# More row maxima computed in the projections of an attention block, and key tiles with W first

## The chip, the cores and the metric

The kernel runs on one core of one Trainium2 chip. The metric is the device time of one execution in microseconds (us), here the median of three runs. A core has TensorE (PE: matmuls; PEld: its weight loads), VectorE (DVE), ScalarE (ACT), GpSimd (POOL), and SyncE (SP), which here only issues DMAs. Each engine works through its own instructions in the order in which the program lists them and waits at semaphores for the others.

## The reference

A transformer block on 2048 tokens of width 640, in float32: attention with 32 heads of width 20, then a gated feed-forward net of width 1728, each behind a layer norm and with a residual.

```
qkv = layernorm(x) @ wqkv                       # 640 x 1920
scores = q @ k.T * 20**-0.5                     # per head, 2048 x 2048
h = x + (softmax(scores) @ v) @ wo
out = h + (silu(z @ w_gate) * (z @ w_up)) @ w_down      # z = layernorm(h)
```

The softmax needs, for every query and head, the maximum of its scores over all 2048 keys. The kernel computes each score twice: once for the maximum alone, with queries as rows, and once for the exponential, with keys as rows.

## The kernel before

Tokens are worked in 4 chunks of 512 (NC), heads in 8 groups of 4 (NG). A unit u = (group g, chunk c) is one group's heads for the 512 queries of one chunk; there are 32 units.

**Maxima.** A maximum item is (u, kc, t, pair): the queries of unit u, tile t of 128 queries, two heads (pair), against the 512 keys of chunk kc. There are three forms:

- `max_pair` (L171, "wide, direct"): two matmuls, one on rows 0 to 63 and one on rows 64 to 127 of the array, write one two-bank tile ps_wide; VectorE reduces it in one instruction (L180).
- `max_halves` (L182, "wide, of halves"): the keys in it have been stored as second half (256) and difference of the halves. Two matmuls (L188) write ps_wide, ScalarE takes the Relu of one half into the tile "over" (L193), and VectorE adds, reduces and reads its accumulator, twice (L195). max(a, b) is b + relu(a - b), so that VectorE reads half as many columns of scores. The queries and keys are tiles "raw" that are loaded from DRAM for it.
- `max_one` (L200, "single"): one matmul (L204) into ps_max and one reduction (L210) for one head.

`in_projections` (L243) decides which items are computed as wide ones while the projections run: 208 of 1024 pairs. The other 816 pairs, "rest" (L254), become 1632 single ones in attention.

**Projections.** 18 slots for each of 4 chunks (L556 on): 10 "block" slots and 8 "value" slots. A block slot (`query_key`, L437) multiplies 15 times (L443) into a ps_one for 128 columns of keys or queries; `keep` (L468) stores them. `keep` copies from PSUM with ScalarE (L484); for key blocks of chunks 0 and 1 POOL makes the difference of the halves (L486); then `split` (L84) makes the high part with ScalarE (L85) and the low part with POOL (L86). `store` (L431) issues the DMAs of the block before on ScalarE's queue (L434 in the profile's rows). A value slot (`value`, L502) multiplies 15 times with 320 columns (L510); in later value slots `flip` (L410) transposes the next chunk's tokens. Chunks 0 to 2 do keys, queries, values (chunk 0 mixes keys and queries); chunk 3 does keys, values, queries.

`visit(n)` (L366) takes up to n wide maxima from two lists, "urgent" and "early", whose heads are ready; an item of halves is ready two slots after its tiles were loaded. Before, a block slot of chunks 1 to 3 visits one in its middle (L448), and every slot visits three at its end (L583). `stage` (L308) lists the tiles to be loaded, `load_items` (L313) loads them into four buffers, `staged_keys` (L325) makes the list of maxima for one group, chunk and key chunk.

**Attention.** 32 units x 16 key tiles of 128 keys, 512 tiles in all. A tile has four scores (`scores`, L943: matmul L948 into ps_one, exponential L954) and one weighing (`weigh`, L956: eight records at L958, 32 columns of the array for each of four heads), which takes the exponentials of two tiles before. ORDER writes out by hand what a tile issues: s and S are scores on the lower and the upper half of the array's rows, m and M single maxima on these halves, W the weighing with small work that hangs on it (the transposed maxima of a closed unit, `max_finish`, the preparation of weights on POOL, in the last units parts of the output projection). ps_one has four banks here, ps_max three, acc one. Before, ORDER has three entries, with 5, 3 and 2 maxima: 10 in three tiles. When no single maximum is left, a tile is "sSsSW". The maxima of a unit must be closed before its first scores, because the negated maximum rides as two more rows of its queries.

After attention come the rest of the output projection and the feed-forward net, from about 1531 us to the end; the change does not touch them.

Of the kernel before, what the change touches and what calls it, by code (L numbers as in the profile page):

```python
# [37 lines left out]
LOWEST = -3.4028234e38  # L38
GD = G * DH

ORDER = ("SmsSMMsWMm", "SsSmWmMs", "SssMWmS")


@with_exitstack
def tile_block(ctx: ExitStack, tc: tile.TileContext, x, wqkv, wo, wg, wu, wd, out):
# [136 lines left out]
    def max_halves(mx, q, k, pair, t, kc):  # L182


        ps = ps_wide()
        for b in range(2):
            rows = slice(b * ROW, b * ROW + NPART)
            nc.tensor.matmul(  # L188
                ps[:, b, :], q[rows, pair, t * P : (t + 1) * P], k[rows, pair, :],
                start=True, stop=True,  # L190
            )
        over = evp.tile([P, 2, CH // 2], F32, name="over")
        nc.scalar.activation(over, ps[:, :, CH // 2 :], AF.Relu)  # L193
        for b in range(2):
            nc.vector.tensor_tensor_reduce(  # L195
                over[:, b], ps[:, b, : CH // 2], over[:, b], 1.0, LOWEST, ALU.add, ALU.max,
                mx[:, b, pair, t, kc : kc + 1],
            )
# [44 lines left out]
    def in_projections(u, kc, t):  # L243


        g, c = divmod(u, NC)
        if u == 0 or (u == 2 and kc < 2) or (c < 2 and kc == 0):
            return True
        return c == 1 and kc == 1 and t < (2 if g < NG // 2 else 3)

    def moved(u, kc):
        return [t for t in range(TPC) if in_projections(u, kc, t)]
# [23 lines left out]
    with tc.tile_pool(name="pa", bufs=2) as pa:  # L276
# [46 lines left out]
                items[n][3:] = t, slot[0]  # L323

        def staged_keys(g, c, kc):  # L325
            k, q = place[1, g, (c, kc)], place[0, g, c]

            def one(t, pair):
                max_halves(mxs[g * NC + c], items[q][3], items[k][3], pair, t, kc)
                for n in (k, q):  # L330
                    users[n] -= 1
                load_items()

            def ready():
                return all(items[n][3] is not None and slot[0] >= items[n][4] + 2 for n in (k, q))

            pairs = [(t, pair) for t in moved(g * NC + c, kc) for pair in range(2)]
            for n in (k, q):
                users[n] += len(pairs)
            return [(ready, lambda a=a: one(*a)) for a in pairs]  # L340
# [12 lines left out]
        for g in range(1, NG):  # L353
            stage((0, 0), 1, g, 0)
            stage(0, 0, g, 0)
        for g in range(1, NG):
            stage((1, 0), 1, g, 0)
            stage(1, 0, g, 1)
            stage((1, 1), 1, g, 1)
        urgent = [a for kc in range(NC) for a in in_unit(0, kc, 18 * kc + 7)]  # L360
        early = [a for g in range(1, NG) for a in staged_keys(g, 0, 0)]
        early += in_unit(1, 0, 28) + in_unit(1, 1, 28)
        early += [a for g in range(1, NG) for kc in range(2) for a in staged_keys(g, 1, kc)]
        early += in_unit(2, 0, 46) + in_unit(2, 1, 46)

        def visit(n):  # L366
# [70 lines left out]
        def query_key(c, m):  # L437

            z_hi, z_lo = zs[c]
            ps = ps_one()  # L440
            for n, (a, w) in enumerate(((z_hi, w_hi), (z_lo, w_hi), (z_hi, w_lo))):
                for k in range(ND):
                    nc.tensor.matmul(  # L443
                        ps, w[:, k, m * P : (m + 1) * P], a[:, k, :],
                        start=(n == 0 and k == 0), stop=(n == 2 and k == ND - 1),
                    )
                    if n == 1 and k == 3 and c:
                        visit(1)  # L448
            keep(c, m, ps)

        firsts = []

        def first_blocks(*hns):

# [12 lines left out]

        def keep(c, m, ps):  # L468

            e = next_e()  # L470
            which, half, n = 1 - m % 2, CH // 2, CH
            hi, lo = e[:, 0], e[:, 1]
            copy = lo.bitcast(F32)
# [1 line left out]
            if slot[0] < 8:  # L475
                split(ps, hi[:, :CH], lo[:, :CH], nc.vector)
                if which:
                    nc.scalar.activation(over, ps[:, half:], AF.Copy)
                    nc.vector.tensor_tensor(
                        out=over, in0=ps[:, :half], in1=over, op=ALU.subtract  # L480
                    )
                    split(over, hi[:, CH:], lo[:, CH:], nc.gpsimd)
            else:
                nc.scalar.activation(copy[:, :CH], ps, AF.Copy)  # L484
                if which and c < 2:
                    nc.gpsimd.tensor_tensor(  # L486
                        out=over, in0=copy[:, :half], in1=copy[:, half:CH], op=ALU.subtract
                    )
                    n = EW
                split(copy[:, :n], hi[:, :n], lo[:, :n], nc.gpsimd)  # L490
            n = EW if which and c < 2 else CH
            r0 = m // 2 * P
            pieces, r = [], r0
# [8 lines left out]
        def value(c, t, half):  # L502
# [5 lines left out]
            for a, w in ((z_hi, w_hi), (z_hi, w_lo), (z_lo, w_hi)):  # L508
                for k in range(ND):
# [2 lines left out]
                        start=(n == 0), stop=(n == 3 * ND - 1),  # L512
                    )
                    n += 1
            dst = ev[:, half * 4 : half * 4 + 4, : G * VW].rearrange("p g (h w) -> p g h w", h=G)
            nc.scalar.activation(
                dst[:, :, :, :DH], ps.rearrange("p (g h d) -> p g h d", g=4, h=G), AF.Copy
# [38 lines left out]
        for c in range(NC):  # L556
# [7 lines left out]
            for j, (kind, *which) in enumerate(work):  # L564
# [11 lines left out]
                if which:  # L576
# [3 lines left out]
                            keep(0, m, ps)  # L580
                    else:
                        (query_key if kind == "block" else value)(c, *which)
                visit(3)  # L583
                if c == 0 and j == 6:
                    for ev in evs:
                        nc.gpsimd.memset(ev, 1.0)
# [439 lines left out]
    for u in range(NU):  # L1026
# [4 lines left out]
        for kt in range(NT):  # L1031
# [1 line left out]
            ready = [v for v, at in closing.items() if at == now[0]]  # L1033
            probs = [pp.tile([P, 2, CH], F32, name="probs") for _ in range(2)]
            heads = [[0, 2], [1, 3]]
            order = ORDER[now[0] % 3] if singles[0] or singles[1] else "sSsSW"
            for op in order:
                if op in "mM":
                    next_max(int(op == "M"))
# [618 lines left out]
```

## Time and profile before

| | us |
|---|---|
| median of three runs (2119.76 to 2120.84) | 2120.24 |
| the profiled execution | 2118.48 |
| its span | 2116.7 |
| projections, to the first score of attention | 346.26 |
| attention, from there to its last parts | to about 1531 |
| output projection's rest and feed-forward net | from there |

How to read the rows: a group is "line, engine, operation, out<-in, shape, xcount | busy us, mean ns of one | idle time of the engine just before them, and what ended it". Busy time is the union of the instructions' times, so that busy time over count is less than the mean where they overlap. A row of a stretch has its bounds and length, then the busy time and the number of instructions of each engine, the granted clock of TensorE as a share, the DMA engines' share and the GB/s. A row of the order of time has start, length, engine, line, operation, tiles, how many were merged, and in brackets the idle time before and what ended it. "ACTq" is an instruction of ScalarE's sequencer, such as the issue of a DMA. The ends of matmuls are modelled, so that TensorE's busy share counts little; its starts are used.

### The profile page before, as it was taken

Reading aid. Unit: us, or ns where it says so; the run is one execution under the profiler, and the core shown is the slowest. Engines: PE = TensorE matmul, PEld = TensorE weight load, DVE = VectorE, ACT = ScalarE, POOL = GpSimd, SP = SyncE. Lnnn points to the kernel's source line nnn. Section 1 sums busy time; section 2 is a strip of 40 time slices with the busy share of each in tenths; the row PEclk is TensorE's granted clock in tenths of the full one; section 3 lists DMA queues with packets and bytes.
Section 4 is the critical chain, followed back from the end, with each engine's and each line's share of the span. In section 5 each row is a group of like instructions: output and inputs, shape, how many; then the busy total and the mean of one; then the engine's idle time right before and its main releaser. Section 6 shows DMA issues by size and latency. Waiting matters only on the chain.

```text
span 2116.7 us, 36528 instructions
## 1 busy us (share of the span) xinstructions
PE 2077.2 (98%) x12636; PEld 1207.4 (57%) x12636; DVE 1695.8 (80%) x3355; ACT 1381.2 (65%) x2727; POOL 707.1 (33%) x1013
## 2 busy tenths in 40 slices
PE   7989999999999999999999999999999999999999
PEld 5756665333333333333333333335578888888888
DVE  6676767999999999999999999996458766666677
ACT  4645655999999899989999999995753222212221
POOL 2222212234334333443430001001135535663456
PEclk9999999999999999999999999999999999999999
DMA  8564543333342533434332213123137745784542
GB/s 261 182 207 148 164 127 90 118 102 128 118 147 81 173 102 120 159 131 142 123 134 60 48 32 91 36 80 96 35 117 246 276 161 200 287 313 154 187 163 94
DMA packets 194159, 297.95 MB, mean 141 GB/s; under 512 B 46840, under 2 KB 81656, under 8 KB 192952
## 3 DMA queue, kind: packets, MB, share of 16 engines
q1 hardware_dynamic: 180392, 266.77, 38.9%
q10 hardware_dynamic: 13584, 28.85, 4.5%
q8 instruction: 101, 1.65, 0.3%
q14 instruction: 82, 0.67, 0.1%
HBM read 196.44 MB, written 98.30 MB: 139 GB/s over the span
## 4 chain that ended last, share of the span: by engine, by line
PE 89%; DVE 4%; DMA 2%; ACT 2%; POOL 1%; issue 1%; ACTq 1%; SPq 0%; POOLq 0%; DVEq 0%
PE acc L958 24%; PE ps_one L948 15%; PE ps_a L1121 15%; PE ps_max L204 15%; PE ps_b L1215 8%; PE ps_one L443 4%; PE ps_one L510 3%; PE ps_max L686 2%; PE ps_wide L188 1%; PE ps_b L686 1%; DVE mx L180 1%; DVE over L195 1%; DVE mx L210 1%; PE ps_wide L176 1%; ACT over L193 1%
## 5 line engine op out<-in xcount | busy, mean ns | idle before, releaser
L954 ACT ACTIVATE probs<-ps_one 128x512 f32<-128x512 f32 x2048 | 1045.3, 621 | 131.4 <-PE ps_one L948 126.5
L210 DVE TENSOR_REDUCE mx<-ps_max 128x1 f32<-128x512 f32 x1632 | 1021.2, 683 | 95.0 <-PE ps_max L204 53.1
L948 PE MATMUL ps_one<-q_stk,k_stk 62*128 62x512 f32 x2048 | 550.1, 421 | 0.7 <-ACT e L484 0.7
L958 PE MATMUL acc<-probs,v_stk 128*32 128x512 f32 x4096 | 545.2, 604 | 0.3
L204 PE MATMUL ps_max<-k_stk,q_stk 60*128 60x512 f32 x1632 | 540.9, 460 | 2.3 <-DVE mx L210 1.5
L204 PEld LDWEIGHTS ps_max<-k_stk,q_stk 60*128 60x128 f32 x1632 | 230.2, 184 | 427.9 <-DVE mx L210 410.3
L948 PEld LDWEIGHTS ps_one<-q_stk,k_stk 62*128 62x128 f32 x2048 | 299.8, 185 | 81.1 <-ACT probs L954 51.5
L1336 DVE TENSOR_TENSOR tmp<-ps_a,tmp 128x512 f32<-128x512 f32 x208 | 141.3, 690 | 120.2 <-PE ps_a L1121 94.5
L1215 PE MATMUL ps_b<-halves,yp 128*128 128x320 f32 x1032 | 179.4, 308 | 2.0 <-POOL yp L86 1.2
L1215 PEld LDWEIGHTS ps_b<-halves,yp 128*128 128x128 f32 x1032 | 165.1, 188 | 18.6 <-POOL yp L86 1.5
L195 DVE CUSTOM_DVE_ANT_0 over<-ps_wide,over 128x256 f32<-128x256 f32 x296 | 109.7, 420 | 82.1 <-ACT over L193 79.6
L958 PEld LDWEIGHTS acc<-probs,v_stk 128*32 128x32 f32 x4096 | 80.6, 108 | 159.7 <-issue 151.7
L221 POOL CAST both<-neg 128x16 fp32r<-128x16 f32 x32 | 6.6, 208 | 470.1 <-DVE neg L217 237.7
L1121 PE MATMUL ps_a<-t,units 128*128 128x512 f32 x624 | 162.7, 396 | 0.0
L1121 PE MATMUL ps_a<-z,units 128*128 128x512 f32 x516 | 133.8, 394 | 0.0
L1121 PEld LDWEIGHTS ps_a<-t,units 128*128 128x128 f32 x624 | 112.6, 188 | 18.7
L86 POOL TENSOR_TENSOR yp<-y,yp 128x256 fp32r<-128x256 f32 x96 | 60.4, 629 | 188.0 <-ACT yp L85 180.0
L1220 DVE TENSOR_TENSOR h<-ps_b,h 128x320 f32<-128x320 f32 x248 | 110.1, 481 | 7.1 <-PE ps_b L1215 5.4
L193 ACT ACTIVATE over<-ps_wide 128x512 f32<-128x512 f32 x148 | 84.0, 597 | 46.1 <-DVE mx L195 18.6
L1121 PEld LDWEIGHTS ps_a<-z,units 128*128 128x128 f32 x516 | 93.1, 187 | 15.9
L85 ACT ACTIVATE yp<-tmp 128x512 fp32r<-128x512 f32 x40 | 25.3, 632 | 103.3 <-POOL tmp L1208 103.3
L1121 PE MATMUL ps_a<-z,lasts 128*128 128x512 f32 x324 | 92.5, 393 | 0.0
(180 smaller groups left out, 2191.3 us busy)
## 6 DMA issues: line engine op xcount, KB each, us to landing
units<-w_d SPq DMA_DIRECT2D x186, 256.0 KB
w_d<-stage SPq DMA_DIRECT2D x106, 256.0 KB
halves<-j_d SPq DMA_DIRECT2D x70, 320.0 KB
j_d<-stage SPq DMA_DIRECT2D x42, 320.0 KB
k_stk<-k_d SPq DMA_DIRECT2D x64, 160.0 KB
q_stk<-q_d SPq DMA_DIRECT2D x64, 160.0 KB
rb<-r_d SPq DMA_DIRECT2D x32, 256.0 KB
raw<-k_d SPq DMA_DIRECT2D x42, 160.0 KB
```

The lines of the kernel that those rows point to most:

```text
L193: nc.scalar.activation(over, ps[:, :, CH // 2 :], AF.Relu)
L195: nc.vector.tensor_tensor_reduce(over[:, b], ps[:, b, : CH // 2], over[:, b], 1.0, LOWEST, ALU.add, ALU.max, mx[:, b, pair, t, kc : kc + 1],)
L204: nc.tensor.matmul(ps, queries[u][rows, pair, t * P : (t + 1) * P], keys[u // NC][rows, pair, kc * CH : (kc + 1) * CH], start=True, stop=True,
L210: nc.vector.tensor_reduce(mxs[u][:, b, pair, t, kc : kc + 1], ps, axis=AX.X, op=ALU.max)
L443: nc.tensor.matmul(ps, w[:, k, m * P : (m + 1) * P], a[:, k, :], start=(n == 0 and k == 0), stop=(n == 2 and k == ND - 1),)
L948: nc.tensor.matmul(ps, keys[u // NC][rows, p, kt * P : (kt + 1) * P], queries[u][rows, p, :], start=True, stop=True,)
L954: nc.scalar.activation(probs[p][:, b, :], ps, AF.Exp, scale=scale)
L958: nc.tensor.matmul(acc[32 * j : 32 * j + 32, :], values[u // NC][:, kt, j * VW : j * VW + 32], probs[j // 2][:, j % 2, :], start=(kt == 0) ...
L1121: nc.tensor.matmul(ps.rearrange("p (t n) -> p t n", t=TPC), w[k][:, i], z[k][:, :, j], start=(first and m == 0), stop=(last and m == len(n ...
L1215: nc.tensor.matmul(ps, a, b, start=(n == 0), stop=(n == len(pairs) - 1))
L1220: nc.vector.tensor_tensor(out=h, in0=ps, in1=h, op=ALU.add)
L1336: add = lambda out, ps, x: nc.vector.tensor_tensor(out=out, in0=ps, in1=x, op=ALU.add)
```

## The change

It has these parts. `in_projections` takes both first key chunks of each group's chunks 0 and 1: 288 pairs instead of 208, 64 of them direct (before 60) and 224 of halves (before 148). The stage list has four tiles a group for that, with the queries of chunk 0 loaded a second time, and the early list another order. A block slot visits two in its middle; a value slot of chunks 1 to 3 visits one or two after nine of its matmuls; the end of a slot visits three, in slots 10 to 17 four. `keep` no longer calls the split of a block (outside the first slots: high part on ScalarE, low part on POOL) at once, but puts it into a list that is run behind the slot's last visit. "over" has three buffers instead of two. The remaining 736 pairs are 1472 single maxima, and ORDER has two entries with three maxima each: nine in three tiles, in another order, with W at the head. The scratch for dynamic DMA is halved, which makes room in SBUF.

```
-ORDER = ("SmsSMMsWMm", "SsSmWmMs", "SssMWmS")
+ORDER = ("WsSmmSsM", "WSsMMsSm")
...
-        over = evp.tile([P, 2, CH // 2], F32, name="over")
+        over = evp.tile([P, 2, CH // 2], F32, name="over", bufs=3)
...
     def in_projections(u, kc, t):
-        g, c = divmod(u, NC)
-        if u == 0 or (u == 2 and kc < 2) or (c < 2 and kc == 0):
-            return True
-        return c == 1 and kc == 1 and t < (2 if g < NG // 2 else 3)
+        return u == 0 or (kc < 2 and (u % NC < 2 or u == 2))
...
         def staged_keys(g, c, kc):
-            k, q = place[1, g, (c, kc)], place[0, g, c]
+            k = place[1, g, (1, 1) if kc else (c, 0)]
+            q = place[0, g, c if c or not kc else 2]
...
         for g in range(1, NG):
+            stage((1, 1), 1, g, 1)
+            stage(2, 0, g, 0)
+            stage(1, 0, g, 1)
             stage((1, 0), 1, g, 0)
-            stage(1, 0, g, 1)
-            stage((1, 1), 1, g, 1)
...
-        early += in_unit(1, 0, 28) + in_unit(1, 1, 28)
-        early += [a for g in range(1, NG) for kc in range(2) for a in staged_keys(g, 1, kc)]
+        early += staged_keys(1, 0, 1) + in_unit(1, 0, 28) + in_unit(1, 1, 28)
+        early += [
+            a for g in range(1, NG) for c, kc in ((0, 1), (1, 1), (1, 0))[g == 1 :]
+            for a in staged_keys(g, c, kc)
+        ]
...
                     if n == 1 and k == 3 and c:
-                        visit(1)
+                        visit(2)
...
-        firsts = []
+        halved, firsts = [], []
+        def finish_keep():
+            while halved:
+                halved.pop(0)()
...
         def keep(c, m, ps):
-            e = next_e()
+            e, before = next_e(), halved[:]
+            halved.clear()
...
-                    split(over, hi[:, CH:], lo[:, CH:], nc.gpsimd)
+                    halved.append(lambda: split(over, hi[:, CH:], lo[:, CH:], nc.gpsimd))
...
-                split(copy[:, :n], hi[:, :n], lo[:, :n], nc.gpsimd)
+                halved.append(lambda n=n: split(copy[:, :n], hi[:, :n], lo[:, :n], nc.gpsimd))
+            for f in before:
+                f()
...
                     n += 1
+                    if n == 9 and c:
+                        visit(1 + half)
...
-                visit(3)
+                visit(4 if 9 < slot[0] < 18 else 3)
+                finish_keep()
...
-            order = ORDER[now[0] % 3] if singles[0] or singles[1] else "sSsSW"
+            order = ORDER[now[0] % 2] if singles[0] or singles[1] else "sSsSW"
...
-        "TRN2", target_bir_lowering=False, num_devices=1, dynamic_dma_scratch_size=8192
+        "TRN2", target_bir_lowering=False, num_devices=1, dynamic_dma_scratch_size=4096
```

## The prediction

> **What bounds the kernel now.** I read the page first, then the busy time by stretches, then TensorE's order of time.
>
> ```profile
> span 2116.7 us, 36528 instructions
> ...
> PE 89%; DVE 4%; DMA 2%; ACT 2%; POOL 1%; issue 1%; ACTq 1%; SPq 0%; POOLq 0%; DVEq 0%
> ...
> L954 ACT ACTIVATE probs<-ps_one 128x512 f32<-128x512 f32 x2048 | 1045.3, 621 | 131.4 <-PE ps_one L948 126.5
> L210 DVE TENSOR_REDUCE mx<-ps_max 128x1 f32<-128x512 f32 x1632 | 1021.2, 683 | 95.0 <-PE ps_max L204 53.1
> ```
>
> TensorE carries 89% of the chain. An exponential occupies ScalarE for 1045.3/2048 = 0.51 us, a single maximum VectorE for 1021.2/1632 = 0.63 us. The stretches, cut at the ends of the projections' groups of slots (length, then busy time and instructions of PE, PEld, DVE, ACT, POOL, clock, DMA share, GB/s):
>
> ```profile
> 61.36:90.23 28.87, 28.53 (x190) 23.59 (x188) 19.88 (x93) 22.06 (x42) 7.11 (x6) 1.00 0.51 158
> 90.23:150.35 60.12, 53.96 (x230) 33.75 (x229) 39.11 (x163) 30.52 (x51) 18.61 (x15) 1.00 0.68 203
> 150.35:181.00 30.65, 29.63 (x190) 23.66 (x188) 23.44 (x59) 16.53 (x32) 7.77 (x6) 1.00 0.38 120
> 181.00:239.85 58.85, 55.17 (x232) 34.77 (x230) 39.19 (x163) 29.62 (x52) 11.64 (x9) 0.97 0.61 186
> 239.85:269.80 29.95, 28.95 (x190) 23.70 (x188) 19.43 (x99) 22.90 (x44) 7.75 (x6) 1.00 0.50 155
> 269.80:297.14 27.34, 26.24 (x118) 16.77 (x116) 14.85 (x80) 16.68 (x30) 5.19 (x4) 1.00 0.51 148
> 297.14:326.51 29.37, 28.12 (x172) 21.66 (x170) 25.40 (x47) 8.21 (x18) 1.72 (x3) 1.00 0.24 77
> 326.51:346.26 19.75, 19.06 (x85) 14.51 (x84) 7.54 (x7) 5.54 (x10) 5.16 (x4) 1.00 0.48 138
> 346.26:1408.80 1062.54, 1061.27 (x7164) 416.92 (x7164) 978.50 (x1611) 967.54 (x1929) 309.08 (x518) 1.00 0.35 107
> ```
>
> They are, in order: values of chunk 0; blocks and values of chunk 1; blocks and values of chunk 2; keys, values and queries of chunk 3; then attention as far as tile 464. In attention three engines are above 90%, so a lighter load on one is worth only what the next allows. One period of three key tiles on TensorE (start, length, what; a value product, L958, has eight records):
>
> ```profile
> 900.15 1.07 PE L958 MATMUL acc<-probs,v_stk 128*32 128x512 f32 x8
> ...
> 902.05 1.06 PE L958 MATMUL acc<-probs,v_stk 128*32 128x512 f32 x8
> 903.04 0.50 PE L204 MATMUL ps_max<-k_stk,q_stk 60*128 60x512 f32 x2
> 903.38 0.63 PE L948 MATMUL ps_one<-q_stk,k_stk 62*128 62x512 f32 x3
> 903.62 0.49 PE L204 MATMUL ps_max<-k_stk,q_stk 60*128 60x512 f32 x1
> 903.85 0.39 PE L948 MATMUL ps_one<-q_stk,k_stk 62*128 62x512 f32 x1
> 904.17 1.06 PE L958 MATMUL acc<-probs,v_stk 128*32 128x512 f32 x8
> ...
> 906.88 1.07 PE L958 MATMUL acc<-probs,v_stk 128*32 128x512 f32 x8
> ```
>
> Capital and small letters of ORDER use the two halves of the array's rows, and two matmuls of unlike halves start together. From one value product to the next it takes 1.90, 2.12 and 2.71 us: about 0.99 for the product, then 6 matmuls (three on each half) in 0.91, 7 (four and three) in 1.13, and 9 in 1.72. Three tiles take 906.88 - 900.15 = 6.73 us, 2.243 each. The seven are four starts: 0.34 to the second, 0.235 to each further, 0.32 from the last to W. Three such starts make 0.90, and five, which nine matmuls need, 0.34 + 3 x 0.235 + 0.32 = 1.37; I put the other 0.35 down to waiting for banks, since five scores and four maxima stand there in a row. All tiles together:
>
> ```profile
> 351.05:1408.80 1057.75, 494.30 (x3712) 72.92 (x3712) 1.00 0.34 106
> ```
>
> 3712/8 = 464 value products, 1057.75/464 = 2.280 us per tile; the 0.037 over 2.243 belongs to the ends of units.
>
> **The change part by part.** *Attention.* Single maxima go from 1632 to 2 x 816 - 2 x 80 = 1472; at 3 a tile they last 491 tiles, as 1632 at 10/3 lasted 490. The new orders put W first and then seven matmuls, four on one half and three on the other (s S m m S s M, and its mirror). That is the split of the stretch from 903.04 to 904.17, which took 1.13. So every tile should take 0.99 + 1.13 = 2.12 us. Cover: ScalarE needs 4 x 0.51 = 2.04, VectorE 3 x 0.63 = 1.88; both fit, ScalarE closely. W at the head reads exponentials of two tiles before, a whole tile after the last of them was issued, and frees its buffers earlier; I price its move at nothing. The three banks of the maxima come round once a tile, the four of the scores too. Gain: 464 x (2.243 - 2.12) = 57 us, and about 2 in the 27 later tiles that still carry maxima. Ends of units: unchanged (0.037 x 464 = 17 us stay; bounds: all 17 gone, or twice as much). **Attention: -58**, bounds -70 and -40.
>
> *Projections: 80 more wide maxima*, 76 of halves and 4 direct. Price on each engine:
>
> ```profile
> 63.76 0.97 PE L188 MATMUL ps_wide<-raw 60*128 60x512 f32 x6
> 64.66 1.00 PE L510 MATMUL ps_one<-w_hi,z_hi 128*128 128x320 f32 x5
> ```
>
> Three cost TensorE 64.66 - 63.76 = 0.90 us, 0.30 each. On VectorE and ScalarE the same two lines in chunk 2's values, and the direct kind in the groups of the first 500 us:
>
> ```profile
> 239.85:269.80 29.95, 17.94 (x96) 1.00 0.50 155
> ```
> ```profile
> 239.85:269.80 29.95, 13.82 (x25) 1.00 0.50 155
> ```
> ```profile
> L180 DVE TENSOR_REDUCE mx<-ps_wide 128x2 f32<-128x1024 f32 x60 | 69.4, 1218 | 2.0 <-PE ps_wide L176 1.7
> ```
>
> 96 records are 24 maxima: 17.94/24 = 0.75 us of VectorE (L195), 13.82/25 = 0.55 of ScalarE (L193); a direct one 69.4/60 = 1.16 of VectorE. The 80 cost TensorE 80 x 0.30 = 24 us, VectorE 76 x 0.75 + 4 x 1.16 = 62, ScalarE 42. VectorE's busy time over the eight stretches is 188.8 of 284.9 us; with 62 it stays under the stretched time, so TensorE's 24 stands, less what it fills of its own idle time (284.9 less 269.7 busy in the eight, 15 us), and the coupling of three nearly full engines over three ps_wide buffers comes on top.
>
> *Blocks' parts behind the maxima.* A key block's ScalarE rows now:
>
> ```profile
> 106.79 0.60 ACT L484 ACTIVATE v_stk<-ps_one 128x512 f32<-128x512 f32 x1 [0.88 <-PE ps_one L443]
> 108.22 0.84 ACT L85 ACTIVATE v_stk<-v_stk 128x768 fp32r<-128x768 f32 x1 [0.84 <-POOL v_stk L486]
> 108.23 2.19 ACTq L434 DMA_DIRECT2D k_d<-e  x3
> 110.52 1.08 ACT L193 ACTIVATE over<-ps_wide 128x512 f32<-128x512 f32 x2 [1.45 <-DMA k_d<-e]
> ```
> ```profile
> 104.66 0.50 PE L188 MATMUL ps_wide<-raw 60*128 60x512 f32 x2 [1.08 <-DVE mx L195]
> ```
>
> The slot's three maxima were ready soon after 106.8, yet ScalarE reached them at 110.52: it stood 0.84 us for POOL's difference, made the high part (0.84) and issued stores. TensorE then stood in the middle of the next block (1.08 at 104.66 in the slot before). With the split emitted behind the maxima, ScalarE goes from the copy to the stores to the maxima. What is queued behind the late split: POOL's low part, and the next block's store, which needs it; a slot of 5.5 us holds both. What remains late is the issue of stores, still ahead of the maxima. The first block of chunk 1 had no such stall:
>
> ```profile
> 90.23 1.43 PE L443 MATMUL ps_one<-z_hi,w_hi 128*128 128x512 f32 x5
> ...
> 95.39 1.43 PE L443 MATMUL ps_one<-z_hi,w_hi 128*128 128x512 f32 x5
> ```
>
> At its 5.16 us ten would take 52, against 60.12; I credit a part of the 8.
>
> By groups, with extra maxima counted in the changed program's order of instructions (+8, -1, +12, +9, +12, +4, +12, +24): chunk 0 values 8 x 0.30 and some coupling, +3.5; chunk 1 blocks -3 (two slots there find no maximum ready); its values 12 x 0.30 and ScalarE near 4.1 us a slot, +5.5; chunk 2 blocks 9 x 0.30 less the stall, -1; its values +4.5; chunk 3 keys +1.5, values +4, queries, where nothing was, 24 x 0.30 and VectorE's direct maxima, +9. The last six maxima now stand right before attention and hold the banks that its first tiles want: 6 x 0.30 are in the queries' term, VectorE's remaining 6 x 0.75 to 6 x 1.16 I take at +3. **Projections: +27**, bounds +12 (24 paid, 12 of the 15 idle gone, no wait at the handover) and +47 (VectorE's 62, less the 15).
>
> *The rest.* A third "over" buffer lets ScalarE run one maximum further; it is inside the terms above. Seven more query loads of 240 KB go into stretches whose DMA share is 0.38 to 0.68; nothing, with a late load as the other end (inside the +47). The halved scratch for dynamic DMA: the profile's DMA issues stand on SPq and ACTq alone; nothing. By the Trainium skill, DMA: Bandwidth & Descriptors, section SWDGE vs HWDGE vs iDMA, the descriptor rings in SBUF serve DMAs that GpSimd issues, and none does here; no run here shows the ring itself.
>
> **Sum.** -58 + 27 = -31 on the profiled execution's 2118.48 us: 2087.5. The median of the runs, 2120.24, is 1.8 above it, so 2089.
>
> **The rivals.** *A, the forecast*: 2089.
>
> *B, the projections swallow most of it.* 24 and 3, less 13 of the 15 idle: +14, net -44, 2076. For it: 6.2 of the 15 lie in chunk 1's blocks and 3.7 in chunk 2's, where the wait goes. Against: VectorE and ScalarE both gain more load than TensorE.
>
> *C, the projections cost what VectorE pays*: +47, net -11, 2109. For it: VectorE at 25.40 of 29.37 already in chunk 3's values. It would be a slot time over 4.6 us in the value slots.
>
> *D, slower: neighbours on one half of the rows.* The new orders hold "mm" or "MM" in every tile. If the second one's weights cannot load while the first runs, each such place costs a late start. The stretch of nine has two such pairs (SS and MM) and 0.35 us beyond its starts, at most 0.17 a pair. At one a tile, 490 tiles give back 83 us: net +52, 2172. It decides from 31/490 = 0.063 us a tile. Against it: at 903.38 three scores, two of them on one half, and the next start at 903.85, follow at 0.235 as unlike ones do. The Trainium skill speaks for D: TensorE: Matmul & The Clock Gate, Part 3 (The mechanism), has a weight load overlap running matmuls only where the row group differs. The trace disagrees as far as the rows from 903.38 to 904.17 go, and I keep D's chance low for it.
>
> *E, it does not do what it says*: a unit's last maxima close about two tiles later than now, and scores wait for the row that carries them. One us at each of 31 starts of units would take all the gain: 2120.
>
> **How the numbers follow.** A 0.52, B 0.17, C 0.15, D 0.10, E 0.06. Faster by over 0.2% (4.2 us, about what a measurement of this kernel can tell from no change) is below 2116: A, B and C, 0.84; same 0.04; slower 0.12. The range for 8 in 10: 2068 (B with the ends of units cheaper by 8) to 2115 (C with attention at -52).
>
> **What would show it.** From one value product to the next 2.12 us in every tile, not 1.90, 2.12, 2.71; the first 464 near 1001 us. VectorE's share there falls to about 88%, ScalarE's rises to 96%. The first score of attention starts near 370 us, not 346; value slots take about 4.2 us, key blocks under 6. In the key blocks the wait of L193 behind POOL is gone. The forecast is wrong if the step at "mm" or "MM" is over 0.3 us (D), if a bank's wait returns every tile, or if the projections end after 395 us.

## The result, and the profile after

The changed kernel takes 2136.81 us (median of six runs, 2128.59 to 2141.45) against 2120.23 (six runs, 2119.67 to 2121.63): a ratio of 1.0074, 95% interval 1.0053 to 1.0096. It is slower; the forecast was 2089. The profiled execution took 2140.56 us. The lines of its page that answer to those shown of before:

```profile
span 2138.8 us, 36948 instructions
...
PE 82%; DVE 5%; DMA 5%; issue 3%; POOL 2%; ACT 2%; SPq 0%; ACTq 0%; POOLq 0%; DVEq 0%
...
L966 ACT ACTIVATE probs<-ps_one 128x512 f32<-128x512 f32 x2048 | 1059.2, 617 | 69.9 <-PE ps_one L960 46.5
L210 DVE TENSOR_REDUCE mx<-ps_max 128x1 f32<-128x512 f32 x1472 | 924.9, 684 | 133.4 <-PE ps_one L960 96.2
```

TensorE lost seven points of the chain to others, above all to DMA and to "issue", time in which the profile names nothing that it waited for. The exponentials' idle time fell from 131 to 70 us: attention is denser. The same stretches as before, cut at the ends of the groups of slots (length, then busy time and instructions of PE, PEld, DVE, ACT, POOL, clock, DMA share, GB/s):

```profile
61.84:111.25 49.41, 37.23 (x205) 29.35 (x204) 27.84 (x131) 27.74 (x52) 9.79 (x7) 0.90 0.40 124
111.25:168.75 57.50, 54.65 (x227) 35.28 (x226) 37.95 (x151) 27.10 (x47) 18.00 (x14) 0.94 0.71 210
168.75:211.56 42.81, 38.39 (x214) 27.75 (x213) 35.10 (x100) 21.86 (x41) 7.75 (x6) 0.96 0.26 83
211.56:270.77 59.21, 56.88 (x250) 35.24 (x248) 46.35 (x199) 31.88 (x59) 11.60 (x9) 1.00 0.60 176
270.77:311.49 40.72, 38.13 (x214) 27.41 (x212) 28.53 (x148) 30.57 (x57) 7.75 (x6) 0.96 0.43 130
311.49:339.59 28.10, 28.01 (x126) 17.47 (x124) 17.85 (x100) 17.64 (x33) 5.15 (x4) 1.00 0.47 143
339.59:376.86 37.27, 35.14 (x195) 24.57 (x193) 29.25 (x118) 19.90 (x41) 1.71 (x3) 1.00 0.40 130
376.86:411.29 34.43, 29.52 (x133) 17.98 (x132) 28.81 (x76) 13.00 (x24) 6.42 (x5) 0.98 0.44 124
411.29:1428.80 1017.51, 1008.70 (x7007) 400.18 (x7011) 886.12 (x1454) 979.75 (x1925) 306.85 (x517) 0.99 0.36 110
```

| stretch | before | after | change | forecast |
|---|---|---|---|---|
| chunk 0, values | 28.87 | 49.41 | +20.5 | +3.5 |
| chunk 1, blocks | 60.12 | 57.50 | -2.6 | -3 |
| chunk 1, values | 30.65 | 42.81 | +12.2 | +5.5 |
| chunk 2, blocks | 58.85 | 59.21 | +0.4 | -1 |
| chunk 2, values | 29.95 | 40.72 | +10.8 | +4.5 |
| chunk 3, keys | 27.34 | 28.10 | +0.8 | +1.5 |
| chunk 3, values | 29.37 | 37.27 | +7.9 | +4 |
| chunk 3, queries, and the handover | 19.75 | 34.43 | +14.7 | +9 and +3 |
| first score of attention at | 346.26 | 411.29 | +65.0 | +27 |

(The groups add up to 64.5; 0.5 came ahead of them.)

The values alone take +51.4 where +17.5 was forecast. In them TensorE is idle for 12.2 us of chunk 0's 49.41, where before it was 0.3 of 28.87. Attention, by the 464 value products (L970) as before:

```profile
415.24:1428.38 1013.14, 495.63 (x3712) 72.89 (x3712) 1.00 0.37 110
```

It takes 1013.14 instead of 1057.75: -44.6 (forecast -57). From product 464 to the end it is +2.5. With 0.8 less from the first score to the first product, 65.0 - 0.8 - 44.6 + 2.5 = 22.1, the difference of the spans.

**Where attention gained.** One tile on TensorE, from W to W:

```profile
902.58 1.06 PE L970 MATMUL acc<-probs,v_stk 128*32 128x512 f32 x8
903.58 0.73 PE L960 MATMUL ps_one<-q_stk,k_stk 62*128 62x512 f32 x3
903.92 0.73 PE L204 MATMUL ps_max<-k_stk,q_stk 60*128 60x512 f32 x3
904.38 0.40 PE L960 MATMUL ps_one<-q_stk,k_stk 62*128 62x512 f32 x1
904.71 1.06 PE L970 MATMUL acc<-probs,v_stk 128*32 128x512 f32 x8
```

904.71 - 902.58 = 2.13: the four starts of the forecast (0.34, two steps of 0.23, 0.33 to W), with "mm" and "MM" neighbours in every tile. 464 x 2.12 are 983.7; 29.5 us are left over. 12.0 of them lie in four stretches that before did not have (7.3, 3.5, 4.2 and 5.5 us from one product to the next). Of the other 17.5, where 17 was forecast for the ends of units, 15.9 lie in 66 tiles of 2.2 to 2.7 us, nearly all of them at ends and starts of units.

**Where attention lost.** The waits of its 464 tiles that did not stand there before (engine, waiting line, waited-for line: us, times, longest):

```profile
PEld ps_one L229 <- POOL both L222: 18.2, 11, 4.8
...
PE ps_one L229 <- POOL both L222: 8.8, 3, 3.9
```

and POOL's order of time at one of these places:

```profile
1064.11 0.88 POOL L868 TENSOR_TENSOR sums<-raw 128x320 f32<-128x320 f32 x1 [16.68 <-DMA raw<-in_B_w_down]
1065.57 0.87 POOL L869 TENSOR_TENSOR sums<-raw,sums 128x320 f32<-128x320 f32 x1 [0.58 <-DMA raw<-in_B_w_down]
1066.40 1.27 POOL L1005 TENSOR_TENSOR o<-o,rb 128x512 f32<-128x512 f32 x1
...
1069.51 0.22 POOL L222 TENSOR_TENSOR both<-neg,both 128x16 fp32r<-128x16 f32 x1
```

L222 splits the finished maxima of a unit, 0.2 us of work; TensorE's transposes (L229) need it. POOL works in order and had stood 16.68 us for a weight load of the later net, so that `both` came behind three more sums and a product (L1005). The transposes hang on W, and W now stands at the head of its tile: they fall due most of a tile earlier. The tile at 1065.6 took 5.5 us for 2.12. TensorE's matmuls stood 8.8 us in three such waits; the fourth stretch, 3.5 us from 788.9, has no such wait, but it lies behind the longest of them, and TensorE's clock stood at half there (from 785.1 to 791.9).

**Where the projections lost.** A value slot of chunk 0 in its steady state, first TensorE, then ScalarE (in brackets the idle time before and what ended it):

```profile
77.60 0.99 PE L519 MATMUL ps_one<-w_hi,z_hi 128*128 128x320 f32 x5
...
80.00 0.96 PE L188 MATMUL ps_wide<-raw 60*128 60x512 f32 x6
82.14 0.50 PE L188 MATMUL ps_wide<-raw 60*128 60x512 f32 x2 [1.18 <-DVE mx L195]
...
82.98 0.98 PE L519 MATMUL ps_one<-w_hi,z_hi 128*128 128x320 f32 x5
```
```profile
80.10 0.44 ACT L527 ACTIVATE ev<-ps_one 128x320 f32<-128x320 f32 x1 [1.74 <-PE ps_one L519]
...
80.59 1.58 ACT L193 ACTIVATE over<-ps_wide 128x512 f32<-128x512 f32 x3
```

Four maxima stand at the end of the slot, and ps_wide has three buffers. Three pairs (six matmuls) go out; the fourth needs the first buffer back, which takes the slot's own copy on ScalarE (0.44), then a Relu, then VectorE's pass. TensorE stands 1.18 us, since the fourth is next in its order, and 82.98 - 77.60 = 5.38 us pass where 3.67 did. Over the whole group, the idle time ahead of L188, in the changed kernel and in the kernel before:

```profile
  ACT over L193: 18.2, 12
  DVE mx L195: 6.3, 4
...
```
```profile
...
  ACT ev L516: 0.6, 1
  DVE mx L195: 0.3, 1
```

(us and times, of the matmuls and of their weight loads added up.) No entry there is a DMA, so late loads of staged tiles are not what held these slots. These are the waits that the forecast put at "some coupling".

### The profile page after: what moved, and what is told of

It is laid out like the page before. It is cut to its first block, busy times and chain, and to the rows that moved or that the text cites. A ratio compares the mean times of both kernels' runs of the same rounds, so it can differ in the third digit from the quotient of the medians.

```text
span 2138.8 us, 36948 instructions
## 1 busy us (share of the span) xinstructions
PE 2073.5 (97%) x12636; PEld 1212.7 (57%) x12636; DVE 1663.6 (78%) x3503; ACT 1432.6 (67%) x2803; POOL 705.0 (33%) x1013
## 3 DMA queue, kind: packets, MB, share of 16 engines
q10 hardware_dynamic: 13584, 28.85, 4.5%
## 4 chain that ended last, share of the span: by engine, by line
PE 82%; DVE 5%; DMA 5%; issue 3%; POOL 2%; ACT 2%; SPq 0%; ACTq 0%; POOLq 0%; DVEq 0%
PE acc L970 22%; PE ps_one L960 14%; PE ps_a L1133 14%; PE ps_max L204 11%; PE ps_b L1227 7%; PE ps_one L445 4%; PE ps_wide L188 3%; PE ps_one L519 3%; DVE mx L180 2%; PE ps_max L698 2%; DVE over L195 1%; PE ps_b L698 1%; DMA k_d<-e 1%; DMA raw<-in_B_w_down 1%; ACT over L193 1%
## 5 line engine op out<-in xcount | busy, mean ns | idle before, releaser
L966 ACT ACTIVATE probs<-ps_one 128x512 f32<-128x512 f32 x2048 | 1059.2, 617 | 69.9 <-PE ps_one L960 46.5
L210 DVE TENSOR_REDUCE mx<-ps_max 128x1 f32<-128x512 f32 x1472 | 924.9, 684 | 133.4 <-PE ps_one L960 96.2
L960 PE MATMUL ps_one<-q_stk,k_stk 62*128 62x512 f32 x2048 | 587.6, 452 | 2.9 <-DVE mx L180 2.9
L970 PE MATMUL acc<-probs,v_stk 128*32 128x512 f32 x4096 | 547.4, 607 | 0.0
L960 PEld LDWEIGHTS ps_one<-q_stk,k_stk 62*128 62x128 f32 x2048 | 252.0, 185 | 428.7 <-ACT probs L966 397.1
L204 PE MATMUL ps_max<-k_stk,q_stk 60*128 60x512 f32 x1472 | 380.0, 426 | 1.4 <-DVE mx L210 1.3
L204 PEld LDWEIGHTS ps_max<-k_stk,q_stk 60*128 60x128 f32 x1472 | 271.5, 187 | 29.2 <-DVE mx L210 4.1
L195 DVE CUSTOM_DVE_ANT_0 over<-ps_wide,over 128x256 f32<-128x256 f32 x448 | 162.1, 420 | 91.1 <-ACT over L193 90.2
L970 PEld LDWEIGHTS acc<-probs,v_stk 128*32 128x32 f32 x4096 | 80.6, 108 | 177.1 <-issue 168.6
L193 ACT ACTIVATE over<-ps_wide 128x512 f32<-128x512 f32 x224 | 122.0, 599 | 69.8 <-PE ps_wide L188 44.2
L188 PE MATMUL ps_wide<-raw 60*128 60x512 f32 x448 | 93.1, 467 | 22.8 <-DVE mx L195 11.6
L1005 POOL TENSOR_TENSOR o<-o,rb 128x512 f32<-128x512 f32 x31 | 39.9, 1286 | 212.5 <-DMA q_stk<-q_d 106.4
L1133 PEld LDWEIGHTS ps_a<-z,units 128*128 128x128 f32 x516 | 93.1, 187 | 15.9
```

The costliest lines, as they stand in the source:

```text
L188: nc.tensor.matmul(ps[:, b, :], q[rows, pair, t * P : (t + 1) * P], k[rows, pair, :], start=True, stop=True,)
L195: nc.vector.tensor_tensor_reduce(over[:, b], ps[:, b, : CH // 2], over[:, b], 1.0, LOWEST, ALU.add, ALU.max, mx[:, b, pair, t, kc : kc + 1],)
L204: nc.tensor.matmul(ps, queries[u][rows, pair, t * P : (t + 1) * P], keys[u // NC][rows, pair, kc * CH : (kc + 1) * CH], start=True, stop=True,
L210: nc.vector.tensor_reduce(mxs[u][:, b, pair, t, kc : kc + 1], ps, axis=AX.X, op=ALU.max)
L960: nc.tensor.matmul(ps, keys[u // NC][rows, p, kt * P : (kt + 1) * P], queries[u][rows, p, :], start=True, stop=True,)
L966: nc.scalar.activation(probs[p][:, b, :], ps, AF.Exp, scale=scale)
```

## The experiments

The theories. **P**: a burst of more maxima than ps_wide has buffers makes TensorE wait for ScalarE and VectorE; the number of maxima a slot does not, if the bursts are short. **L**: VectorE and ScalarE have no room for the added load, wherever it stands. **Q**: attention's lost 12 us are the wait for `both` behind POOL's other work. Others are named in the expectations. The kernel before was run beside each: 2121.24 us (13 runs) beside the first four kernels below, 2120.31 (23) beside the next four, 2121.3 (19) beside the last two.

**1. Three instead of four at the ends of chunk 0's value slots.**

```
-                visit(4 if 9 < slot[0] < 18 else 3)
+                visit(3)
```

> The changed kernel, with three wide maxima instead of four at the end of the slots 10 to 17 (chunk 0's values); the eight that are left move to later slots and to the end of the projections. Theory P (a burst's fourth maximum waits until VectorE gives back one of the three ps_wide buffers): chunk 0's values fall from 49.4 us to about 32, the end of the projections grows by 6 to 9, the whole is 8 to 12 us below the changed kernel. Theory L (VectorE and ScalarE have no room for the load): 8 x 0.75 = 6 us leave these slots and come back at the end; chunk 0's values near 43, the whole unchanged within 4 us.

2128.13 us (2127.98 to 2132.93), ratio 1.0038 (1.0023 to 1.0053). Chunk 0's values take 28.85 us instead of 49.41, at a granted clock of 1.00. Eight maxima fewer, 20.6 us less, 2.6 for each where the forecast had 0.44. The idle time ahead of L188 there is that of the kernel before again:

```profile
  issue: 1.5, 8
  ACT ev L527: 0.6, 1
  DVE mx L195: 0.3, 1
```

P holds, and more strongly than it expected (about 32 us); L falls, which expected 43 and no change of the whole. The whole is about 8 us below the changed kernel, at the edge of P's 8 to 12. Part of the 20.6 comes back in chunk 1, whose blocks took 64.2 with one slot of 12.8.

**2. The same number of maxima in the value slots, in two bursts of at most two or three.**

```
-                    if n == 9 and c:
-                        visit(1 + half)
+                    if n == 7:
+                        visit(2)
...
-                visit(4 if 9 < slot[0] < 18 else 3)
+                visit(3 if kind == "block" or slot[0] < 10 else 2 + (c > 0 and which[-1]))
```

> The changed kernel, with the same number of wide maxima in every slot, but in value slots two after seven of the fifteen matmuls and two or three at the end, instead of four at the end (chunk 0) or one or two after nine and three at the end. Theory P: bursts of two or three find their buffers free; chunk 0's values go from 49.4 us to 33 to 36, those of chunks 1 to 3 from 120.8 in all to 100 to 108; the whole is 25 to 35 us below the changed kernel, near 2105. Theory L: the load is the same; within 5 us of the changed kernel.

2124.43 us (2120.87 to 2128.16), ratio 1.0018 (1.0009 to 1.0028): 12 faster than the changed kernel, less than expected. Chunk 0's values take 35.37, inside P's bounds, with all 32 maxima in. One slot:

```profile
78.61 0.97 PE L519 MATMUL ps_one<-w_hi,z_hi 128*128 128x320 f32 x5
...
79.80 0.73 PE L188 MATMUL ps_wide<-raw 60*128 60x512 f32 x4
80.47 0.71 PE L519 MATMUL ps_one<-w_lo,z_hi 128*128 128x320 f32 x3
...
81.84 0.73 PE L188 MATMUL ps_wide<-raw 60*128 60x512 f32 x4
...
82.91 0.97 PE L519 MATMUL ps_one<-w_hi,z_hi 128*128 128x320 f32 x5
```

82.91 - 78.61 = 4.30 with four maxima and no wait. A burst of two takes 80.47 - 79.80 = 0.67 us, one of three 0.90 (the prediction's row at 63.76), so each further maximum in a burst costs about 0.23 and opening a burst about 0.2 (worked out from these two). The chunks 1 to 3 missed their 100 to 108: 40.46 + 37.73 + 36.81 = 115.0, from 120.8. What remains there is not the fourth maximum alone.

**3. The split of a block called at once again**, the rest of the change left.

```
-                    halved.append(lambda: split(over, hi[:, CH:], lo[:, CH:], nc.gpsimd))
+                    split(over, hi[:, CH:], lo[:, CH:], nc.gpsimd)
...
-                halved.append(lambda n=n: split(copy[:, :n], hi[:, :n], lo[:, :n], nc.gpsimd))
+                split(copy[:, :n], hi[:, :n], lo[:, :n], nc.gpsimd)
```

> The changed kernel, with a block's split emitted at once in keep, as before the change, and not behind the slot's maxima. Theory P with the forecast's step on blocks: the blocks of chunks 1 and 2 (116.7 us) grow by 6 to 12, the first value slot of chunk 0 (8.7) and the one behind it, in which a store waited for the late low part ahead of the maxima, shrink by 2 to 4; the whole is 3 to 9 us slower than the changed kernel. Theory L: ScalarE's sum of work is the same, no change within 4 us.

2142.8 us (2139.44 to 2145.21), ratio 1.01 (1.0085 to 1.0115): 6 slower than the changed kernel by the medians, as expected, though the intervals of the ratios overlap. The blocks of chunks 1 and 2 grew by only 1.7 (118.4 for 116.7) and chunk 3's keys by 2.5, not the 6 to 12 that were expected of the blocks: chunk 1's fourth slot, which waits for a load, happened to be 2.9 shorter and hid as much. Chunk 0's values became shorter, and this row tells more than the expectation asked:

```profile
62.87:105.67 42.80, 33.44 (x205) 25.85 (x204) 26.76 (x131) 26.92 (x51) 7.86 (x6) 1.00 0.41 131
```

At full clock throughout, eight slots with a burst of four take 42.80, 13.9 more than before: 1.74 a slot, the steady slot above. So of the +20.5, 13.9 is the burst. Of the other 6.6, 4.9 is in the first two slots (8.7 and 7.0 in the changed kernel, 5.6 and 5.2 here) and 1.7 in the sixth and seventh, where the clock stood at half from 99.0 to 102.4. The late split and a slower clock are both in the 4.9: in experiment 4, which leaves the slots of the projections as the changed kernel has them, the same two slots took 6.5 and 6.4, and the group 44.91 at a clock of 0.96.

**4. `both` on VectorE instead of POOL.**

```
-        nc.gpsimd.tensor_copy(ends[u][:, 0], neg)
-        nc.gpsimd.tensor_tensor(
+        nc.vector.tensor_copy(ends[u][:, 0], neg)
+        nc.vector.tensor_tensor(
```

> The changed kernel, with the two small operations that make the negated maximum's high and low part on VectorE instead of POOL. Theory Q (TensorE's transposes at W, now at the head of the tile, wait for POOL, which stands in front of a late load of weights): the gaps of 7.3, 4.2 and 5.5 us between value products vanish, tiles 0 to 464 take 999 to 1002 us instead of 1008.9 to 1013, the whole is 8 to 12 us below the changed kernel and its runs lie closer together. Rival: the gaps come from DMA of queries and keys itself, and stay; no change within 3 us.

2134.2 us (2127.95 to 2135.28), ratio 1.0055 (1.0037 to 1.0073): 2.6 below the changed kernel, not 8 to 12, and with overlapping intervals not told from it. The 464 tiles:

```profile
409.34:1420.01 1010.67, 494.74 (x3713) 72.94 (x3713) 1.00 0.37 111
```

No wait for `both` is left, and the four long stretches with their 12.0 us are gone; but the 464 tiles are only 2.5 us shorter, so about 9.6 came elsewhere. At ends of units VectorE's two extra instructions stand between single maxima, and tiles of 2.7 to 3.4 us appear there: the weight loads of single maxima wait for VectorE for 12.7 us in 34 places, in the changed kernel for 1.1 in 7. Q is right about the wait, and this cure costs nearly what it saves.

**5. Experiment 2's kernel, and the transposes of a closed unit due one tile later.**

```
-                closing[a[0]] = now[0] + 2
+                closing[a[0]] = now[0] + 3
```

> The kernel with spread value slots, and a unit's negated maximum transposed three tiles after its last maximum instead of two. Theory Q (the transposes at the head of the tile wait for POOL, which stands before a load): the gaps of 7.3, 5.0 and 5.7 us and the ones behind them (16 us beyond 2.12 in six tiles) vanish without new work on VectorE; tiles 0 to 464 take about 1001 us instead of 1017, the whole about 12 to 16 us below the kernel with spread value slots. Rival: three tiles are too late for the scores that wait for the row, and gaps come back at the starts of units 3, 7, 11 and so on; no gain or a loss.

2115.09 us (2110.28 to 2118.56), ratio 0.998 (0.9967 to 0.9992): 8 (by the ratios) to 9 faster than experiment 2, of 12 to 16 expected. The tiles:

```profile
392.85:1400.35 1007.50, 495.55 (x3713) 72.91 (x3713) 1.00 0.37 111
```

from 1017.34 in experiment 2; expected was about 1001. Nothing but the due time changed, so Q is shown: most of the wait goes when the transposes stand a tile further behind what POOL has to do. One gap of 5.3 us stays, where POOL stood 20.4 us for a load.

**6. Experiment 2's kernel, with direct maxima and maxima of halves mixed.** The list "urgent" holds the direct ones. A visit takes one of them at its head, and after that a direct one only when no maximum of halves is ready (the lists are filled to match, which is left out here):

```
-            for _ in range(n):
-                for queue in (urgent, early):
+            for i in range(n):
+                for queue in (early, urgent) if i else (urgent, early):
```

> The kernel with spread value slots, and at most one direct maximum (1.16 us of VectorE) at the head of each visit, the others of halves (0.75), instead of runs of direct ones. Theory D2 (what is left over in the value slots of chunks 1 to 3 and at the end are runs of direct maxima, which VectorE works off at 1.16 us each through three buffers): the first four value slots of chunk 1 go from 6.2, 6.5, 4.5, 5.7 to under 5, the last slot from 12.1 to under 10; the projections end near 373 us instead of 385, the whole is 8 to 14 us below the kernel with spread value slots. Rival (VectorE's total is what counts): within 4 us.

2120.31 us (2112.37 to 2123.17), ratio 0.9993 (0.9979 to 1.0007): 4 to 5 faster than experiment 2, less than expected. Values of chunks 1 to 3 take 38.23 + 36.69 + 35.82 = 110.7 (115.0 before this edit), the queries 32.29 instead of 34.46. A run of direct maxima (1.16 us of VectorE each) was part of what remained, about 6 us of it. The first score came at 390.9, though, not near 373: in this profile chunk 1's blocks took 60.9, with a slot of 12.8, and chunk 0's values 38.8, against 53.8 and 35.4 in experiment 2's.

**7. Experiments 2, 5 and 6 together.**

> Spread value slots, mixed direct maxima and the transposes a tile later, together. If Q and D2 both hold, their gains add: 2095 to 2103 and faster than the kernel before by about 1%. If one of them falls, near 2110; if both, 2124.

2110.38 us (2103.0 to 2112.61), ratio 0.9952 (0.9934 to 0.997): faster than both kernels, by 0.5% and 1.2%, though over the 2095 to 2103 expected. The profile is of the run of 2103.0. Chunk 1's blocks and the tiles:

```profile
96.90:151.64 54.74, 52.21 (x228) 33.74 (x226) 38.10 (x161) 29.14 (x51) 18.07 (x14) 1.00 0.74 223
385.94:1390.38 1004.44, 1001.58 (x6990) 398.09 (x6989) 883.38 (x1449) 971.70 (x1918) 307.51 (x517) 1.00 0.37 112
```

First score at 382.05 (35.8 later than before), attention 53.3 shorter. 288 wide maxima do pay, at this distribution; of the 10 us, about 4 are what the late split gives by itself (experiment 9).

**8. The changed kernel with ORDER of before**, and single maxima taken only from units up to two ahead.

```
-ORDER = ("WsSmmSsM", "WSsMMsSm")
+ORDER = ("SmsSMMsWMm", "SsSmWmMs", "SssMWmS")
...
-        if singles[b]:
+        if singles[b] and singles[b][0][0] <= now[0] // NT + 2:
...
-            order = ORDER[now[0] % 2] if singles[0] or singles[1] else "sSsSW"
+            order = ORDER[now[0] % 3] if singles[0] or singles[1] else "sSsSW"
```

> The changed kernel with its 1472 single maxima, but in the order of before (5, 3 and 2 in three tiles, W in the middle), and a single maximum only for units up to two ahead; where none is allowed, a tile carries none. The forecast's step (a tile of seven matmuls is four starts, 2.12 us, while the order of before makes three tiles of 6, 7 and 9 with 0.35 us of waiting in the last): about 440 tiles at 2.24 and 48 short ones near 1.95, tiles 0 to 464 about 30 to 45 us longer than in the changed kernel. Rival (the gain in attention comes from the number of maxima alone): within 8 us of the changed kernel.

2168.71 us (2167.55 to 2171.03), ratio 1.0233 (1.0215 to 1.0252).

```profile
413.24:1461.49 1048.25, 495.14 (x3713) 72.95 (x3713) 1.00 0.34 107
```

With the same 1472 singles the old order takes 35.1 us more for the 464 tiles, inside the 30 to 45 expected; the rival (within 8) falls. The gain of attention is the order's (its mix and W's place together); 160 fewer maxima by themselves give 9.5 of the 44.6. And with W back in the middle, the waits of these tiles have none of L229 for `both`. But nine in three tiles can only be written because they are fewer.

**9. The kernel before with the late split alone.** Its edit is the change's lines of `halved` and `finish_keep`, nothing else.

> The kernel before with one part of the change alone: the split of a block runs behind the slot's last maxima. Lists of maxima, visits, ORDER and the two over buffers stay as before. Theory S (ScalarE's wait for POOL's difference, ahead of the maxima, was what held the key blocks): chunk 1's blocks go from 60.1 to 56 to 58 us, chunk 2's from 58.9 to 57 to 58, chunk 3's keys and queries, which have no difference, stay within 0.5; the first value slot behind each group of blocks gets up to 2 longer. The whole is 2 to 4 us faster than before. Rival V (the blocks of the changed kernel became shorter because two maxima are visited in the middle, so that fewer stand at the end): the blocks stay within 1 us of before, and the whole within 1 us or, by the stores of the first value slots, 2 to 4 slower.

2116.43 us (2114.21 to 2120.69), ratio 0.9979 (0.9969 to 0.9988). Chunk 1's and 2's blocks:

```profile
89.80:146.81 57.01, 53.77 (x230) 33.62 (x228) 41.25 (x163) 29.28 (x51) 18.60 (x15) 1.00 0.70 214
...
178.60:236.83 58.23, 55.09 (x232) 34.39 (x231) 41.36 (x163) 28.63 (x51) 11.60 (x9) 0.97 0.62 188
```

57.01 instead of 60.12 is inside S's bounds. 58.23 instead of 58.85 is just over them, and by itself would suit V as well; chunk 3's keys gained 0.9, where S allowed 0.5. The last line of L193's waits in chunk 1's blocks, who waited for it, here and in the kernel before:

```profile
  PEld ps_wide L188: 2.2, 4
```
```profile
  PEld ps_wide L188: 6.2, 5
```

S is shown for chunk 1, where V falls, since nothing moved but the split. The price is there too: the first value slot of chunk 0 took 5.0 instead of 3.3, and its group grew by 1.2; the last block's split and stores now stand ahead of that slot's maxima, which is the likely cause. The values of chunks 1 to 3 grew by 1.1, 0.8 and 1.0, so that what the projections gain from chunk 0's values on is only 0.6 us; 1.6 came ahead of them, where kernels of the same code differ by more (chunk 0's values start between 59.5 and 62.2 in the changed kernel and experiments 1, 4 and 8). The gain of the whole is measured; where all of it comes from is not.

**10. Experiment 2's kernel with two "over" buffers.**

```
-        over = evp.tile([P, 2, CH // 2], F32, name="over", bufs=3)
+        over = evp.tile([P, 2, CH // 2], F32, name="over")
```

> The kernel e2_spread_values with two over buffers instead of three. If ScalarE's lead over VectorE is what a burst of maxima lives on (theory O), value slots with two bursts of two stay as they are, since two buffers hold a burst, but the blocks' bursts of three at the end get longer: the key blocks of chunks 1 and 2 by 0.3 to 0.6 us a slot, 6 to 10 in all, and the whole by as much. If the three ps_wide buffers alone set the burst (theory P), a third over buffer gives nothing: every group within 1 us of e2 and the whole within 3 us.

2126.11 us (2121.06 to 2131.82), ratio 1.0024 (1.0012 to 1.0036): 1.7 more than experiment 2, with overlapping intervals. Value slots with two bursts of two still take 4.3. Seven of the eight groups are within about 1 us, but chunk 2's blocks are 2.4 longer, with the clock at half for 3.4 us in them, chunk 0's values start 1.8 later, and the first score comes 7.8 later in all; attention's tiles are 3.2 shorter. The blocks of chunks 1 and 2 are 3.4 longer together, not O's 6 to 10. P's reading of the whole holds (within 3); a small part of the third buffer cannot be told from the spread of one profile each.

## Why the prediction was wrong

**Attention: right in mechanism, short by 12 us.** The 464 tiles gained 44.6 where 57 stood. The tile is 2.12, what lies outside the four stretches 17.5 (forecast 17), VectorE's share 886.12/1017.51 = 87% and ScalarE's 96%, as forecast. The failed sentence is "I price its move at nothing", of W to the head: with W the small work that hangs on it moved too, and L229 came ahead of POOL's turn. The price was 12.0 us, 8.8 of them plain waits at three places. It is near rival E in that the end of a unit waits, but E's reason, maxima that close late, is not what the rows show. Experiments 4 and 5 show the cause, and in experiment 8, with W in the middle, the waits are absent.

**D fell.** Same-half neighbours start 0.23 apart, and tiles with such a pair take 2.12 to 2.13 us throughout. The second maximum's weights load at 903.92, while the first still runs (903.92 to 904.31, by its modelled end). The rule that spoke for it (the Trainium skill, TensorE: Matmul & The Clock Gate, Part 3, The mechanism) isn't what these traces show for two matmuls of 60 rows on the same half.

**Projections: +65 where +27 stood; this step turned the sign.** The failed term is the price of a maximum, 0.30 us of TensorE "and some coupling", worst for chunk 0's values (+3.5; +20.5 came). 0.30 is a third of a burst of three, the most that three buffers take without a wait for a buffer of the same burst. The price of the fourth was never read, and the totals that should have bounded it could not: VectorE is busy for 27.84 of chunk 0's 49.41 us, ScalarE for 27.74. No engine is full; each waits for the next once a slot. So also the upper bound, +47 by VectorE's load, was no bound, and B and C fell with the forecast, since all three priced engines. The projections ended after 395 us, which the prediction gave as a sign against itself; value slots took 4.7 to 6.2 us on the mean of a chunk, not 4.2. By parts:

- The burst of four: 13.9 us in chunk 0 (experiment 3's row at full clock against before); eight fewer take away all 20.6 (experiment 1).
- Values of chunks 1 to 3, +30.8 for +14: spreading gives back 5.8 (experiment 2), mixing the direct ones 4.3 (experiment 6). The +20.8 that stay (110.74 for 89.97) are for 36 more maxima, 0.58 each, near the 0.63 of experiment 2's slots in chunk 0 (4.30 for 3.67). In experiment 6 TensorE is idle for 5.3 us of these groups, in the kernel before for 3.3. So about 2 of the 20.8 are waits, and I take most of the rest for the price of opening a second burst; no run varies that price alone.
- Queries with the handover, +14.7 for +12: nearly right, and the mechanism was the one named. Six direct maxima are left for the end, three buffers:

```profile
407.85 0.49 PE L176 MATMUL ps_wide<-k_stk,q_stk 60*128 60x512 f32 x2 [0.63 <-DVE mx L180]
411.29 0.89 PE L960 MATMUL ps_one<-q_stk,k_stk 62*128 62x512 f32 x2 [2.94 <-DVE mx L180]
```

- The blocks: -2.6 and +0.4 for -3 and -1, 5.75 and 5.92 us each, under 6 as said. Right: experiment 9 shows the cause alone for chunk 1, and the late split is the one part of the change that was tried by itself and pays (0.2%).

**What stays open.** In chunk 1's fourth block slot TensorE stood for a staged load; that slot took 7.6 us before, 10.5 in the changed kernel, 6.0 to 12.8 in the others, and no experiment moved a load. The changed kernel's six runs spread over 13 us, and their times go with the granted clock, 0.990 at 2139 to 2141 us and 0.995 at 2128.59. The clock's share in the result is open too. By the stretches of the last section, TensorE's clock stood at half for 41 us against 6.8 before; if it was busy in all of them, it lost half of that, which would be at most 17 of the 22 us that the profile is longer, and in chunk 0's values, at a clock of 0.90, at most 5 of 20.5 (estimates from these figures).

## What to carry to other kernels

Price one more unit of work by the place where it is issued: count the buffers that a burst needs against those there are, and read a slot's chain (here copy, Relu, VectorE, then TensorE) before any engine's total of busy time. An instruction in order behind slow loads, like POOL's 0.2 us for `both`, is as late as the load; moving its consumer forward by part of a tile can be what makes it felt. Where an edit has several parts, the smallest (here the late split) may be the one to keep, and the others pay only after they are spread out.

## What the runs showed of the hardware that was not expected

A wait of TensorE can cost more than its length. In the first value slot of the changed kernel's chunk 0, TensorE was busy for 0.63 of 3.40 us; then for two stretches of 3.4 its clock stood at half (columns as above, by stretches; then TensorE's order of time):

```profile
64.90:68.30 3.40, 0.63 (x4) 0.21 (x2) 2.71 (x6) 1.45 (x4) 1.27 (x1) 1.00 0.85 221
68.30:71.70 3.40, 1.85 (x6) 1.45 (x7) 2.50 (x13) 2.17 (x4) 0.00 (x0) 0.50 0.59 157
71.70:75.10 3.40, 3.40 (x15) 3.07 (x15) 0.96 (x5) 0.12 (x1) 0.00 (x0) 0.50 0.00 0
```

```profile
70.57 1.70 PE L519 MATMUL ps_one<-w_hi,z_hi 128*128 128x320 f32 x5
...
74.87 1.08 PE L188 MATMUL ps_wide<-raw 60*128 60x512 f32 x6
```

The slot's 15 matmuls take 74.87 - 70.57 = 4.30 us; at full clock, in the slot shown further up, 80.00 - 77.60 = 2.40. The changed kernel has eight such stretches of 3.4 or 6.8 us, about 41 us in all, before two of 3.4, experiment 7 three (13.7 us); the last microseconds of every profile are left out. The Trainium skill, TensorE: Matmul & The Clock Gate, Part 1 (A second HAM failure mode: psum-queue depth-cycling), tells of a kernel that cycles through its PSUM banks and in which TensorE is idle for short times between groups of matmuls often enough that its clock goes back and forth between half and full. The trace agrees in kind. But such waits do not always do it: experiment 3 had the same burst of four in every slot of chunk 0's values, with waits of about 1.1 us, and its clock stayed at 1.00 there. No run here changed the clock alone.
